# Fused decode step on Trainium2: TensorE's code begins behind 350 products that never run, and 256 rows of W_down go to 32 partitions by four small transfers

## The chip, the cores and the metric

The kernel runs on one core of one Trainium2 chip. The metric is the device time of one execution in microseconds; lower is better. A core has five engines that follow their own instruction streams: TensorE (PE, with its weight loads listed apart as PEld), VectorE (DVE), ScalarE (ACT), GpSimd (POOL) and SyncE (SP), and 16 DMA engines that move data between the chip's memory (HBM) and the on-chip buffer.

## The reference

One decode step for four sequences (B = 4, one token each, D = 512). A layer norm of x feeds two branches that are added to x.

```python
xn = _layernorm(x)
q = xn @ wq                      # 32 heads of 128, 8 key/value heads
scores = q @ k^T * Dh**-0.5      # the last 4096 positions of k_cache
o = softmax(scores) @ v
A = o.reshape(B, 1, 4096) @ wo
B_ = (silu(xn @ w_gate) * (xn @ w_up)) @ w_down   # F = 1792
return x + A + B_
```

All inputs are bfloat16. The 4,096 positions of 8 key/value heads and 4 sequences make 64 MiB of keys and values; the weights add 13 MiB.

## The kernel before, in words

**Transfers.** SP issues nearly every transfer, in one queue, in this order (L256 to L267): wq into the second V buffer, w_gate, w_up, then for each of the 8 key/value heads g the keys K(g) and the values V(g), 4 MiB each, into two buffers that take turns; the keys of the last head come in two halves. Behind V(7) come the transfers of W_down (L261 to L263), and behind these wo in five parts of 16, 8, 5, 2 and 1 row blocks (L265, L266). A transfer over 128 partitions is split over all 16 DMA engines, and its semaphore is complete when the last of them has landed its share. K(g) waits until the transposes of K(g-2) are done, V(g) until the products of V(g-2) are done; wo goes into the first K buffer once head 6's transposes are done.

**W_down.** F is 14 blocks of 128 rows. 13 of them (`NM = NF - 1`) go to `WD`, 128 partitions of 13 KiB, by one transfer (L261). The remaining 128 rows go to `WDX`, which lies where w_gate was: 16 partitions (`JX = 128 // NX`) with `NX = 8` rows each, by four transfers of four partitions, `WDX[o:JX:4]` for o = 0 to 3 (L262, L263). Each partition takes 8 KiB. TensorE waits for all five with one wait (L483) and multiplies the 13 blocks in `down` (L482) and the 8 rows of each of 16 partitions in `down_rest` (L487).

**TensorE's code.** It is written out instruction by instruction and follows this order: 4 transposes of xn (L377), 128 products for q (L384), 84 products for the gate and 84 for the up projection (L396; NM + NX = 21 groups of NC = 4), then a loop over pairs of heads (L491) whose body holds both heads of a pair, then the tail (L523 to L545). A product is two instructions, a weight load and a multiplication. The code holds about 1,080 products: 300 ahead of the loop, 696 in the loop's body, 84 in the tail. The loop runs four times.

**A head in the loop.** 16 chunks of 8 transposes of K (L415), evicted by DVE (L326) and ACT (L280), 16 chunks of 8 score products (L427), the maximum (L332 to L340), its subtraction (L439), the exponential on ACT (L283), and the products with V (L448, L454). `spin` (L468) issues products whose result nobody reads; `warm` calls it in the gaps at the softmax.

**The tail.** `fin` (L459) closes the last head; `down`; four products that permute the result (L528), which wait for DVE's `norm` (L345 to L352); `down_rest`; then wo. Its first 16 row blocks go into four row groups of one bank (L538), which ACT copies (L298); the other 16 go straight into the result (L540), each part after the wait for its transfer (L535). DVE and ACT copy the result (L370, L300) and ACT's queue stores it (L302).

Of the kernel before, what the change touches and what calls it, by code (L numbers as in the profile page):

```python
# [10 lines left out]
def bass_parallel_sum__sliding_block_cached__swiglu_ffn__decode_kernel(  # L11
# [12 lines left out]
    B, _, D = A_x.shape  # L24
    _, HKV, Sk, Dh = A_k_cache.shape
# [5 lines left out]
    NF = F // 128  # L31
# [15 lines left out]
    WOS = (0, 16, 24, 29, 31, 32)  # L47
    WOE = 16
    NR = HQ * Dh // 128

    NM = NF - 1
    FM = 128 * NM
    NX = 8
    JX = 128 // NX

    def sb(name, shape, dtype, align=32):
        return nc.alloc_sbuf_tensor(name, shape, dtype, align_bytes=align)
# [8 lines left out]
    WU = sb("wu_sb", [128, NC, F], BF16, 512)  # L66
    WD = sb("wd_sb", [128, NM, D], BF16, 512)
    WO = KB[0][:].rearrange("p t d -> p (t d)").rearrange("p (r n) -> p r n", r=NR)

    WDX = WG[0:JX].rearrange("p c f -> p (c f)")[:, 0:NX * D].rearrange("p (m n) -> p m n", n=D)  # L70
    X = sb("x_sb", [B, D], BF16, 512)
# [22 lines left out]

    OP = sb("oP", [128, NR, 32], BF16)
    S2 = sb("s2", [128, D], FP32)
    ex = sb("ex", [128, NM + NX, B], FP32)
    gs = sb("gs", [128, NM + NX, B], FP32)
    guT = sb("guT", [128, NM + NX, 32], BF16)
    ident = sb("ident", [128, 128], BF16)  # L100
    ones = sb("ones", [128, 128], BF16)
    I4 = sb("i4", [B, B], FP32)
    own = sb("own", [128, 128], BF16)
# [3 lines left out]
    dq = sb("dq", [128, 4], FP32)  # L107
    dr = sb("dr", [128, NR], BF16)
    sel = sb("sel", [128, 32], FP32)
# [4 lines left out]
    ps_kt = [ps("ps_kt%d" % s, [128, 512], FP32) for s in range(3)]  # L114
# [12 lines left out]
    q_ps = ps_S[0][:, 0:HQ * B]  # L127
    gate_ps = ps_O[:, 64:64 + (NM + NX) * B].rearrange("p (t b) -> p t b", b=B)
    up_ps = ps_O[:, 192:192 + (NM + NX) * B].rearrange("p (t b) -> p t b", b=B)
# [3 lines left out]
    acc4_ps = ps_S[1]  # L133
    perm_ps = [ps_kt[h][:, 0:B // 2 * NR] for h in (2, 0)]

# [49 lines left out]
    wdx_ap = B_w_down[0:F - FM].rearrange("(i o m) n -> o i m n", o=4, m=NX)  # L185
    wo_ap = A_wo.rearrange("(p r) n -> p r n", r=NR)

# [47 lines left out]
    def on_sync(eng):  # L235
# [26 lines left out]
        for o in range(4):  # L262
            eng.dma_start(WDX[o:JX:4], wdx_ap[o]).then_inc(d_wd, 16)  # L263
        eng.wait_ge(s_tr[NCH - 1], HKV - 1)
# [106 lines left out]

    def on_tensor(eng):
        mm = eng.matmul
        eng.wait_ge(s_const, 1)
        eng.wait_ge(s_xn, 1)
        for c in range(NC):
# [10 lines left out]
        for w, d, o in ((WG, d_wg, gate_ps), (WU, d_wu, up_ps)):  # L387
            eng.wait_ge(d, 16)
            for t in range(NM + NX):
                for c in range(NC):  # L390
                    if t < NM:
                        left = w[:, :, F - FM:F].rearrange("p c (m t) -> p c t m", t=NM)[:, c, t, :]
                    else:
# [4 lines left out]
                              skip_group_check=True)  # L398
# [60 lines left out]
        def fin(n):  # L459
# [4 lines left out]
                last = mm(O2_ps, Osb[:, Dh * h:Dh * (h + 1)], sel[:, NH * h:NH * (h + 1)],  # L464
                          start=(h == 0), stop=(h == 1), skip_group_check=True)
            last.then_inc(s_fin, 1)

        def spin(n, k=2):  # L468
            for _ in range(n):
                mm(ps_kt[k][:], ones[:], own[:].unsqueeze(1).to_broadcast([128, 4, 128]),  # L470
                   skip_group_check=True)

        def acc4(n, left, right, start, stop):
            return mm(acc4_ps[32 * n:32 * n + 32, :], left, right, start=start, stop=stop, skip_group_check=True)  # L474
# [12 lines left out]
        def down_rest():  # L487
            for m in range(NX):
                acc4(m % 4, guT[0:JX, NM + m, :], WDX[:, m, :], False, False)

        with eng.Fori(1, HKV + 1, 2) as m:  # L491

            d = eng.snap((m - 1) * 8 + 16)
            for u in range(2):
                n = m if u == 0 else eng.snap(m + 1)
                n1 = eng.snap(n + 1)

                def warm(k, bank=2):

                    if u:  # L500
                        spin(k, bank)
                    else:
                        with eng.If(m > 1):
                            spin(k, bank)
                for c in range(NCH):
                    transposes(u, c, n, d)
                    if c == 2:
                        fin(n)
                    if c >= 2:
                        scores(c - 2, n)  # L510
                scores(NCH - 2, n)
                scores(NCH - 1, n)
                warm(5)
                maxima(n)
                warm(5)
                shift(n)
                eng.wait_ge(d_v[u], d)
                pv(u, n1)
                if u == 0:
                    with eng.If(m < HKV - 1):  # L520
                        warm(4, 1)

        spin(2, 1)  # L523
        fin(HKV + 1)
        down()
        eng.wait_ge(s_nrm, HKV + 1)
        for b in range(B):
            last = mm(perm_ps[b // 2][:, NR * (b % 2):NR * (b % 2 + 1)], OT[:, b, 2:HKV + 2].rearrange("p k h q -> p (k h q)"), dr[:])  # L528
        last.then_inc(s_pm, 1)
# [22 lines left out]
    on_scalar(nc.scalar)  # L552
    on_vector(nc.vector)
    on_tensor(nc.tensor)

# [26 lines left out]
```

## Time and profile before

| | |
|---|---|
| median of 3 runs | 195.12 us (195.11 to 195.25) |
| the profiled execution's own time | 195.3 us |
| its span in the trace | 193.9 us |
| granted TensorE clock | 0.991 |
| PE busy / DVE / ACT | 163.8 / 99.0 / 69.1 us |
| HBM read | 81.01 MB, 418 GB/s over the span |
| DMA packets of data on SP's queue | 3776 |
| DMA packets of instructions | 8 |

The span runs from the first to the last instruction that the trace holds; 1.4 us of the execution lie around it. In the DMA view a window of the trace lists the packets that start in it, and how many of them are under 512 B. Each of the DMA engines that serve a transfer ends its share with a packet of 4 B, the write of the semaphore; the count under 512 B in a short window is therefore the number of engines that end a transfer there.

### The profile page before, as it was taken

How to read it: one execution, taken by the hardware profiler on the slowest of the kernel's cores; microseconds unless marked ns; L12 is line 12 of the kernel's file. 1: busy time of each engine (PE TensorE's matmuls, PEld its weight loads, DVE VectorE, ACT ScalarE, POOL GpSimd, SP SyncE). 2: the span in 40 equal slices, each digit the busy share in tenths (PEclk: the TensorE clock that was granted, in tenths of full speed). 3: DMA queues.
4: the chain of work that ended last, by engine and by line, in shares of the span. 5: the costliest groups of instructions: out<-in, count | busy, mean ns of one | idle time of the engine just before them, and what ended most of it. 6: DMA issues, size and time to landing. Idle time of an engine off the chain costs nothing.

```text
span 193.9 us, 6951 instructions
## 1 busy us (share of the span) xinstructions
PE 163.8 (84%) x3179; PEld 135.2 (70%) x3179; DVE 99.0 (51%) x200; ACT 69.1 (36%) x100; POOL 5.7 (3%) x33
## 2 busy tenths in 40 slices
PE   0038973998699899999999799989996999999995
PEld 0038973997389759956994699469945994997532
DVE  0200011578258737870885188428842884588230
ACT  5510000243416343525461446234623462363421
POOL 7300000000000000000000000000000000000000
PEclk9999999999789999999999999999999999999999
DMA  6999999999999999999999999999999999999993
GB/s 216 433 438 429 427 429 433 429 433 429 433 429 436 426 429 436 426 433 433 439 433 433 433 433 433 433 433 433 433 433 433 433 426 433 439 433 433 436 400 131
DMA packets 3800, 81.14 MB, mean 418 GB/s; under 512 B 440, under 2 KB 576, under 8 KB 832
## 3 DMA queue, kind: packets, MB, share of 16 engines
q1 hardware_dynamic: 3776, 81.00, 97.5%
q8 instruction: 8, 0.13, 0.2%
q10 hardware_dynamic: 16, 0.01, 0.0%
HBM read 81.01 MB, written 0.00 MB: 418 GB/s over the span
## 4 chain that ended last, share of the span: by engine, by line
PE 48%; DMA 44%; DVE 5%; issue 1%; SPq 1%; ACT 0%; DVEq 0%
DMA kbuf<-in_A_k_cache_dram 44%; PE ps_kt L415 23%; PE ps_s L427 8%; PE ps_o L448 5%; PE ps_kt L470 4%; DVE kT L326 2%; PE ps_s L439 2%; PE ps_s L464 2%; DVE mx L332 2%; PE ps_s L478 1%; PE ps_s L474 1%; PE ps_s L461 1%; PE ps_kt L454 1%; PE ps_kt L434 0%; ACT s L298 0%
## 5 line engine op out<-in xcount | busy, mean ns | idle before, releaser
L415 PE MATMUL ps_kt<-ident,kbuf 128*128 128x128 bf16 x1024 | 78.2, 224 | 9.0 <-DMA kbuf<-in_A_k_cache_dram 8.5
L415 PEld LDWEIGHTS ps_kt<-ident,kbuf 128*128 128x128 bf16 x1024 | 60.6, 100 | 11.2 <-DMA kbuf<-in_A_k_cache_dram 9.6
L326 DVE COPY kT<-ps_kt 128x1024 bf16<-128x1024 bf16 x88 | 57.6, 686 | 18.5 <-PE ps_kt L415 16.5
L280 ACT ACTIVATE kT<-ps_kt 128x1024 bf16<-128x1024 bf16 x40 | 40.9, 1023 | 52.9 <-PE ps_kt L415 52.9
L427 PE MATMUL ps_s<-qC,kT 128*128 128x16 bf16 x1024 | 44.8, 170 | 2.6 <-DVE kT L326 1.9
L427 PEld LDWEIGHTS ps_s<-qC,kT 128*128 128x128 bf16 x1024 | 38.4, 97 | 4.6 <-DVE kT L326 4.1
L283 ACT ACTIVATE p<-ps_s 128x512 bf16<-128x512 f32 x32 | 16.5, 603 | 34.0 <-PE ps_s L439 34.0
L332 DVE TENSOR_REDUCE mx<-ps_s 128x16 f32<-128x512 f32 x32 | 22.0, 689 | 6.9 <-PE ps_s L427 5.0
L470 PE MATMUL ps_kt<-own,ones 128*128 128x512 bf16 x82 | 20.7, 380 | 0.0
L448 PE MATMUL ps_o<-vbuf,p 128*32 128x256 bf16 x512 | 19.1, 289 | 0.3
L448 PEld LDWEIGHTS ps_o<-vbuf,p 128*32 128x32 bf16 x512 | 14.9, 101 | 5.9 <-ACT p L283 4.2
L343 DVE TENSOR_REDUCE dsum<-ps_kt 128x16 f32<-128x256 f32 x8 | 3.4, 425 | 28.6 <-PE ps_kt L454 28.6
L454 PE MATMUL ps_kt<-p,ones 128*32 128x256 bf16 x64 | 16.9, 287 | 0.0
L470 PEld LDWEIGHTS ps_kt<-own,ones 128*128 128x128 bf16 x82 | 6.6, 97 | 7.0 <-issue 1.1
L377 PE MATMUL ps_s<-i,xn 4*128 4x4 f32 x4 | 0.6, 254 | 10.1 <-DVE xn L312 10.1
L439 PE MATMUL ps_s<-cm,own 128*128 128x512 bf16 x32 | 8.3, 380 | 1.0 <-DVE cm L340 1.0
L377 PEld LDWEIGHTS ps_s<-i,xn 4*128 4x128 f32 x4 | 0.6, 208 | 10.1 <-issue 10.1
L454 PEld LDWEIGHTS ps_kt<-p,ones 128*32 128x32 bf16 x64 | 6.6, 103 | 0.1
L290 ACT ACTIVATE ex<-ps_o 128x84 f32<-128x84 f32 x1 | 0.2, 240 | 17.5 <-PE ps_o L396 17.5
L439 PEld LDWEIGHTS ps_s<-cm,own 128*128 128x128 bf16 x32 | 2.5, 97 | 5.3 <-DVE cm L340 3.4
L286 ACT ACTIVATE osb<-ps_o 128x256 f32<-128x256 f32 x8 | 3.1, 383 | 8.2 <-PE ps_kt L454 8.2
L464 PE MATMUL ps_s<-sel,osb 128*128 128x16 f32 x36 | 5.8, 275 | 0.0
(83 smaller groups left out, 84.8 us busy)
## 6 DMA issues: line engine op xcount, KB each, us to landing
vbuf<-in_A_v_cache_dram SPq DMA_DIRECT2D x8, 4096.0 KB, 30.5
kbuf<-in_A_k_cache_dram SPq DMA_DIRECT2D x7, 4096.0 KB, 27.4
vbuf<-in_A_wq_dram SPq DMA_DIRECT2D x1, 4096.0 KB, 12.4
kbuf<-in_A_k_cache_dram SPq DMA_DIRECT2D x2, 2048.0 KB, 25.3
kbuf<-in_A_wo_dram SPq DMA_DIRECT2D x1, 2048.0 KB, 27.2
wg_sb<-in_B_w_gate_dram SPq DMA_DIRECT2D x1, 1792.0 KB, 16.1
wu_sb<-in_B_w_up_dram SPq DMA_DIRECT2D x1, 1792.0 KB, 20.9
wd_sb<-in_B_w_down_dram SPq DMA_DIRECT2D x1, 1664.0 KB
```

Of the source, the lines that this page charges most:

```text
L280: eng.activation(KT[:, c % 4], kt_ps[c % 3], ACT.Copy).then_inc(s_ev[c], 1)
L283: eng.activation(P[:, BT * q:BT * (q + 1), :], ps_S[q][:].rearrange("p (t n) -> p t n", n=NH), ACT.Exp, scale=SCALE).then_inc(s_p[q], 1)
L326: eng.tensor_copy(KT[:, c % 4], kt_ps[c % 3]).then_inc(s_ev[c], 1)
L332: eng.tensor_reduce(mx[:, q, :], ps_S[q][:].rearrange("p (t n) -> p n t", n=NH), AX.X, ALU.max)
L343: eng.tensor_reduce(dsum[:], den_ps.rearrange("p (t n) -> p n t", n=NH), AX.X, ALU.add).then_inc(s_dn, 1)
L415: last = eng.transpose(kt_ps[c % 3][:, k, :], KB[u][:, CH * c + k, :], ident[:])
L427: last = mm(ps_S[q][:, NH * t:NH * (t + 1)], KT[:, c % 4, k, :], QC[:], start=(t == 0), stop=False, skip_group_check=True)
L439: mm(ps_S[q][:].rearrange("p (t n) -> p t n", n=NH), own[:], CM[:].unsqueeze(1).to_broadcast([128, BT, NH]), start=False, stop=True, skip_ ...
L448: mm(O_ps[32 * n:32 * n + 32, :], P[:, t:t + 2, :].rearrange("p t n -> p (t n)"), VB[u][:, t:t + 2, :].rearrange("p t d -> p (t d)"), star ...
L454: last = mm(den_ps[32 * n:32 * n + 32, :], ones[:, 0:32], P[:, DT * e:DT * (e + 1), :].rearrange("p t n -> p (t n)"), start=(e < 4), stop= ...
L464: last = mm(O2_ps, Osb[:, Dh * h:Dh * (h + 1)], sel[:, NH * h:NH * (h + 1)], start=(h == 0), stop=(h == 1), skip_group_check=True)
L470: mm(ps_kt[k][:], ones[:], own[:].unsqueeze(1).to_broadcast([128, 4, 128]), skip_group_check=True)
```

## The change

- 256 rows of W_down instead of 128 go to `WDX`: `NM` falls from 13 to 12, `JX` rises from 16 to 32. `WD` takes 12 KiB on each of 128 partitions; each of the four small transfers now has 8 partitions of 8 KiB. The bytes in all are the same.
- The groups of the gate and up projections fall from 21 to 20 (80 products each instead of 84), those of `down` from 13 to 12; `down_rest` keeps 8 products, on 32 partitions instead of 16.
- TensorE's code begins with a register set to 0, a branch on it, and `ROOM = 350` products that the branch jumps over: 700 instructions that never run. `spin` is defined ahead of them instead of further down. All code behind them lies 700 odd instructions further on.

```diff
-    NM = NF - 1
+    ROOM = 350
+
+    NM = NF - 2
     FM = 128 * NM
     NX = 8
-    JX = 128 // NX
+    JX = 256 // NX
...
     def on_tensor(eng):
         mm = eng.matmul
+
+        def spin(n, k=2):
+            for _ in range(n):
+                mm(ps_kt[k][:], ones[:], own[:].unsqueeze(1).to_broadcast([128, 4, 128]),
+                   skip_group_check=True)
+
+        zero = eng.alloc_register("never")
+        eng.reg_mov(zero, 0)
+        with eng.If(eng.snap(zero) > 0):
+            spin(ROOM)
         eng.wait_ge(s_const, 1)
```

More of the change, by code (lines that the diff above doesn't have):

```diff
@@ L466, in fin @@
             last.then_inc(s_fin, 1)
[L468 to L471, printed above, removed]
         def acc4(n, left, right, start, stop):
```

## The prediction

> **What bounds the kernel now.** I read the page's slices and queues first, then the chain of waits, then the DMA view in windows. From the page:
>
> ```profile
> span 193.9 us, 6951 instructions
> ...
> GB/s 216 433 438 429 427 429 433 429 433 429 433 429 436 426 429 436 426 433 433 439 433 433 433 433 433 433 433 433 433 433 433 433 426 433 439 433 433 436 400 131
> DMA packets 3800, 81.14 MB, mean 418 GB/s; under 512 B 440, under 2 KB 576, under 8 KB 832
> ...
> q8 instruction: 8, 0.13, 0.2%
> ```
>
> The transfers run at 433 GB/s from the first slice to the last but one, 27.1 GB/s for each of 16 DMA engines; nothing that only makes an engine faster can shorten that. Eight packets of 16 KB are instructions. The chain of waits, and the one wait of the tail that matters:
>
> ```profile
> 0.81 0.39 SPq L256
> ...
> 83.81 26.45 DMA kbuf<-in_A_k_cache_dram
> ...
> 120.96 28.01 DMA kbuf<-in_A_k_cache_dram
> 149.01 1.51 PE ps_kt L415 x24
> ...
> 189.61 2.54 PE ps_s L478 x36
> ...
> PEld ps_s L478 <- DMA kbuf<-in_A_wo_dram: 0.4, 2, 0.2
> ```
>
> PE waits for keys until 110.3 and again until 149.0; from there it works almost without a gap into the last products of wo (L478), and there it waits for wo twice, 0.4 us in all. So the end hangs on two things of nearly equal length: the last landing of wo, after which only L478's last pair, the copy and the store are left, and PE's own work since 149.0, which is at most 0.4 us shorter. A later last landing moves the end one to one; an earlier one can win 0.4 us at most.
>
> The last landing is that of the slowest of 16 DMA engines, so I ask how far they lie apart. The instruction queue in the windows 15 to 28, 28 to 40 and 15 to 80 us, a row from each:
>
> ```profile
> q8 instruction: 2, 0.03, 0.9%
> q8 instruction: 1, 0.02, 0.5%
> q8 instruction: 8, 0.13, 0.7%
> ```
>
> All eight come between 15 and 80 us, while PE goes through its code for the first time, none in the later passes: fetched code stays. About 2,230 instructions (1,080 products of two, and some 70 others) in the eight blocks fetched and a first one or two present at the start make some 220 to 250 a block of 16 KB. Then how many engines end a transfer in a window (the count under 512 B): wq in 12.1 to 12.6 and 12.6 to 12.9; V(0) in 40.0 to 40.5, 41.5 to 41.8 and 42.1 to 42.2; V(7) in 175.6 to 176.0, 176.0 to 177.1, 177.1 to 177.5 and 177.6 to 177.8; wo's first part in 184.5 to 184.8, 185.7 to 186.3 and 186.5 to 186.6; a row from each:
>
> ```profile
> DMA packets 30, 0.22 MB, mean 430 GB/s; under 512 B 15, under 2 KB 15, under 8 KB 15
> DMA packets 11, 0.14 MB, mean 478 GB/s; under 512 B 1, under 2 KB 1, under 8 KB 1
> DMA packets 28, 0.49 MB, mean 983 GB/s; under 512 B 13, under 2 KB 13, under 8 KB 13
> DMA packets 8, 0.20 MB, mean 655 GB/s; under 512 B 2, under 2 KB 2, under 8 KB 2
> DMA packets 2, 0.03 MB, mean 328 GB/s; under 512 B 1, under 2 KB 1, under 8 KB 1
> DMA packets 19, 0.20 MB, mean 512 GB/s; under 512 B 8, under 2 KB 8, under 8 KB 8
> DMA packets 21, 0.38 MB, mean 343 GB/s; under 512 B 0, under 2 KB 0, under 8 KB 0
> DMA packets 22, 0.20 MB, mean 499 GB/s; under 512 B 7, under 2 KB 7, under 8 KB 7
> DMA packets 11, 0.13 MB, mean 666 GB/s; under 512 B 1, under 2 KB 1, under 8 KB 1
> DMA packets 16, 0.16 MB, mean 546 GB/s; under 512 B 4, under 2 KB 4, under 8 KB 4
> DMA packets 37, 0.22 MB, mean 369 GB/s; under 512 B 11, under 2 KB 11, under 8 KB 11
> DMA packets 11, 0.08 MB, mean 819 GB/s; under 512 B 1, under 2 KB 1, under 8 KB 1
> ```
>
> This carries everything that follows. Before any fetch the engines end wq together, one of them, call it S, some 0.3 us behind. After three fetches three engines are 1.4 us late at V(0), and the last of them, alone at 42.1, is S: the third fetch was on S. After eight fetches eight engines are late by 1.4 us, S last again. So each fetch holds up one engine, each a different one, by **1.4 us, and it is never made good**, for no engine is ever idle. Behind the W_down transfers only four engines are still early: the four small transfers lie on four engines without a fetch. The page's 440 packets under 512 B say so too: 26 transfers on 16 engines (416), x and the output on 4 each (8), which leaves 16 for four transfers, 4 engines each. 32 KB more on these four cost them 1.2 us, which just filled their lead.
>
> **The change, part by part.**
>
> *W_down.* Durations are of the profiled execution (195.3 us, span 193.9, so 1.4 us around it; the median of the runs is 0.2 us lower).
>
> ```profile
> wd_sb<-in_B_w_down_dram SPq DMA_DIRECT2D x1, 1664.0 KB
> ...
> wg_sb<-in_B_w_down_dram SPq DMA_DIRECT2D x4, 32.0 KB
> ```
>
> The large transfer becomes 1,536 KB: 8 KB less on each engine, 8 / 27.1 = -0.30 us. The small ones become 64 KB each. By the pattern of four partitions on four engines I take eight on eight: 32 KB on each of eight engines, +1.21 us, four of them new. No row shows eight; what another spread would do is a rival.
>
> *The code.* PE jumps over 700 instructions, some three blocks, as soon as the kernel begins; SP, which starts with it, issues its first transfer at 0.81 us (row above), so I put the jump at about 1 us. The block it lands in, and the next, were not fetched before, since the blocks present at the start lie at the front. So they are fetched at once, between about 1 and 6 us. PE itself loses nothing:
>
> ```profile
> PE ps_s L377 <- DVE xn L312: 10.1, 1, 10.1
> ...
> PEld ps_kt L528 <- DVE oT L352: 0.4, 1, 0.4
> ...
> 0.00:1.80 1.80, 0.00 (x0) 0.00 (x0) 0.00 (x0) 0.00 (x0) 1.08 (x14) 1.00 0.00 0
> 1.80:2.20 0.40, 0.00 (x0) 0.00 (x0) 0.00 (x0) 0.00 (x0) 0.22 (x2) 1.00 3.60 983
> ```
>
> It waits for xn until 10.1 us anyway. Without that cover a stall of one fetch, a few us, would be paid once. But the data stream begins at 1.8 to 2.2 us, so the two fetches meet it. Their price is the unknown: nothing, if they get in ahead; 16 KB at 27.1 GB/s, 0.61 us; or 1.4 us as for the eight others. I take 1.4, the row it is nearest to: two more fetches on a busy engine. Then come the fetches of the first pass as before, from the prologue into the tail: some eight. Ten in all instead of eight, and some eight engines with extra rows, on 16 engines: at least two engines have both. The early fetch of the second block lands on S: by block (S's was the third one fetched before, the fifth of the code if two are present at the start; the landing in the fourth makes the fifth the next) as well as by the order of fetches, give or take one.
>
> [...]
>
> *The sum.* S carried one fetch before and carries one after. If it is among the eight: -0.30 + 1.21 = **+0.91 us**. S ended last before, so the end moves by this: span 194.8, the execution 196.2, on the median 195.12 + 0.91 = **196.0 us**. PE's own chain is no help: K(6) on S is as late as before, so head 6 starts at 149.0 again.
>
> *What lies beside other work.* Four gate and four up products fewer end before K(0) has landed. `down` has 12 products instead of 13 while the next step waits 0.4 us for DVE's oT (row above): nothing won. K(0) on S comes some 0.4 us after the other late engines, so head 0 starts later by that; the 26.45 us wait for keys that ends at 110.3 takes it up. SP's four issues stay where they were, 30 us ahead of their landing. Were these covers gone, each would cost 0.1 to 0.4 us.
>
> **The rivals.**
>
> *Another engine than S has both.* The eight engines with a fetch avoided the first four. If they follow each other, there are five places for them, and S lies within the first eight in two. In the other three an engine that ended 0.3 to 0.5 us ahead of S gets the +0.91, or one of the first four trades 8 KB for a fetch: -0.30 + 1.4, from 0.6 to 0.8 us ahead. Both end +0.3 to +0.6: 195.4 to 195.7. [...]
>
> *The early fetches cost half*, 0.61: S then is at -0.30 + 1.21 - 1.4 + 0.6 = +0.1: 195.2, no measurable change.
>
> *The other side: they cost nothing.* Ahead of the stream, an early fetch leaves S without a late one, and if all later ones fall on the eight without extra rows, S moves by -0.30 + 1.21 - 1.4 = -0.5, the others by -0.30. K(6) would land 0.3 earlier too, and PE's chain with it, so about -0.4 of it reaches the end: 194.7. It decides from an early fetch under 0.5 us on S. For it: the branch comes at about 1 us, the stream at 1.8. Against: the jump and the stream's start lie within a microsecond of each other, and S's block is the second to be fetched.
>
> *The change does not do what it says*: the small transfers are spread otherwise (all 16 engines: S -0.30 + 0.61 = +0.3; the same four: +0.1 to +0.3): 195.2 to 195.4.
>
> *The loop's code no longer stays* and is fetched again in each pass: one or more 1.4 us on an engine per pass, over 197.
>
> **How the numbers follow.** A measurement of this kernel tells about 0.2%, 0.4 us, from no change. Chances: S with both 0.36; another engine with both 0.24; half price 0.15; free 0.15; spread otherwise 0.06; fetched in each pass 0.04. Slower by over 0.2%: 0.36 + 0.22 + 0.04 = 0.62. Within: 0.15 + 0.06 + 0.02 + 0.03 of the free case = 0.26. Faster: 0.12. The range takes in the bounds of the early fetch, nothing (194.7) to 1.4 us, with 0.3 us for its size above: 194.7 to 196.3.
>
> **What would show it.** Right: ten or so instruction packets, two of them before 8 us; 456 packets under 512 B on the page; two engines late at wq, one of them S near 14.2; two engines alone at the end of wo, some 0.9 us behind the rest. Wrong: no instruction packet before 15 us, or sixteen engines that end wq within 0.7 us; wo's end with all engines within 0.5 us; packets of instructions after 80 us ahead of the tail.

## The result and the profile after

| | before | after |
|---|---|---|
| median of 6 runs each | 195.19 us (195.11 to 195.35) | 196.3 us (196.15 to 196.34) |
| ratio | | 1.0055 [1.0045, 1.0066] |
| the profiled execution's own time | 195.3 us | 196.34 us |
| its span | 193.9 us | 194.9 us |

The kernel became 1.1 us slower. The page of the changed kernel, its head and its queue of instructions:

```profile
span 194.9 us, 6936 instructions
...
DMA packets 3834, 81.18 MB, mean 416 GB/s; under 512 B 456, under 2 KB 592, under 8 KB 848
...
q8 instruction: 10, 0.16, 0.3%
```

Ten packets of instructions instead of eight, and 456 packets under 512 B instead of 440: each of the four small transfers now ends on eight engines. When the instructions were fetched, by the DMA view of the changed kernel in the windows 0 to 15, 15 to 80 and 80 to 194 us:

```profile
q8 instruction: 2, 0.03, 0.8%
q8 instruction: 7, 0.11, 0.6%
q8 instruction: 1, 0.02, 0.1%
```

Two come ahead of 15 us (at 3.9 and 10.2), seven by the end of the loop's first pass at 73 us (two of these ahead of the loop, whose first products start at 32.7 us), and one in the tail (between 189 and 190 us). The same view tells how many engines end a transfer in a window: wq in 12.0 to 12.9, 13.75 to 13.85 and 14.0 to 14.2; V(7) in 175.5 to 176.3, 177.1 to 177.6 and 178.6 to 178.8; the last part of wo in 191.9 to 192.1 and 192.4 to 192.5 (the count under 512 B):

```profile
DMA packets 35, 0.34 MB, mean 376 GB/s; under 512 B 14, under 2 KB 14, under 8 KB 14
DMA packets 3, 0.03 MB, mean 287 GB/s; under 512 B 1, under 2 KB 1, under 8 KB 1
DMA packets 8, 0.10 MB, mean 502 GB/s; under 512 B 1, under 2 KB 1, under 8 KB 1
...
DMA packets 26, 0.36 MB, mean 456 GB/s; under 512 B 8, under 2 KB 8, under 8 KB 8
DMA packets 26, 0.25 MB, mean 508 GB/s; under 512 B 7, under 2 KB 7, under 8 KB 7
DMA packets 10, 0.11 MB, mean 553 GB/s; under 512 B 1, under 2 KB 1, under 8 KB 1
...
DMA packets 12, 0.01 MB, mean 61 GB/s; under 512 B 2, under 2 KB 10, under 8 KB 12
DMA packets 2, 0.00 MB, mean 10 GB/s; under 512 B 1, under 2 KB 2, under 8 KB 2
```

The first group shows the two early fetches: two engines end wq 1.4 us or so behind the fourteen others. So an early fetch costs what a late one costs. The packets of the trace show what the 1.4 us is made of: a packet of code takes 0.88 to 0.97 us on its engine, and the packet of keys, values or weights right behind it takes 1.67 to 1.76 us instead of 1.21 (32 KB). The second group shows what the prediction did not have. By the end of V(7) nine fetches have come, but eight engines are still early; seven are 1.4 us late and one, alone at 178.7, is late by twice that. The ninth fetch fell on an engine that had been held up already. The packets can be followed engine by engine, for in this full stream a packet starts 3 or 4 ns before the one ahead of it on its engine ends. Followed so, the late one is the engine of the first fetch. The tenth, in the tail, falls on that of the second, and this engine is the last of all at the end of wo, alone at 192.47.

The chain of waits of the changed kernel, for the windows 80 to 195 us:

```profile
83.90 27.32 DMA kbuf<-in_A_k_cache_dram
111.27 1.51 PE ps_kt L426 x24
...
121.93 27.95 DMA kbuf<-in_A_k_cache_dram
149.93 1.51 PE ps_kt L426 x24
...
190.53 2.65 PE ps_s L484 x36
```

L426 and L484 are L415 and L478 of before. Head 6 begins at 149.93 instead of 149.01, for the engine with two fetches lands its share of K(6) last. These +0.92 us stay in PE's chain to the first product of L484: 190.53 instead of 189.61, +0.92. And the waits for wo of the changed kernel:

```profile
PEld ps_s L484 <- DMA kbuf<-in_A_wo_dram: 0.7, 3, 0.2
```

0.7 us instead of 0.4 us, some of it on the path: L484 takes 2.65 us to the end of its run instead of 2.54. So of the 1.0 us by which the span grew, 0.9 were there 30 us before the rows of W_down came, and 0.1 came in the tail.

### The profile page after: what moved, and what is told of

It is laid out like the page before. It is cut to its first block, busy times and chain, and to the rows that moved or that the text cites. A ratio compares the mean times of both kernels' runs of the same rounds, so it can differ in the third digit from the quotient of the medians.

```text
span 194.9 us, 6936 instructions
## 1 busy us (share of the span) xinstructions
PE 162.6 (83%) x3170; PEld 133.5 (69%) x3170; DVE 98.8 (51%) x200; ACT 69.2 (35%) x100; POOL 5.7 (3%) x33
## 4 chain that ended last, share of the span: by engine, by line
PE 48%; DMA 44%; DVE 4%; issue 1%; SPq 1%; ACT 0%; DVEq 0%
DMA kbuf<-in_A_k_cache_dram 44%; PE ps_kt L426 23%; PE ps_s L438 9%; PE ps_o L459 4%; PE ps_kt L378 4%; PE ps_s L450 2%; DVE kT L327 2%; PE ps_s L475 2%; PE ps_s L484 1%; DVE mx L333 1%; PE ps_s L472 1%; PE ps_s L480 1%; PE ps_kt L465 1%; PE ps_kt L445 0%; ACT s L299 0%
## 5 line engine op out<-in xcount | busy, mean ns | idle before, releaser
L426 PE MATMUL ps_kt<-ident,kbuf 128*128 128x128 bf16 x1024 | 77.8, 223 | 9.0 <-DMA kbuf<-in_A_k_cache_dram 8.9
L426 PEld LDWEIGHTS ps_kt<-ident,kbuf 128*128 128x128 bf16 x1024 | 60.2, 99 | 12.4 <-DMA kbuf<-in_A_k_cache_dram 10.5
L459 PEld LDWEIGHTS ps_o<-vbuf,p 128*32 128x32 bf16 x512 | 14.3, 97 | 5.8 <-ACT p L284 4.6
L459 PE MATMUL ps_o<-vbuf,p 128*32 128x256 bf16 x512 | 18.0, 278 | 0.3
L465 PE MATMUL ps_kt<-p,ones 128*32 128x256 bf16 x64 | 15.9, 276 | 0.0
L450 PE MATMUL ps_s<-cm,own 128*128 128x512 bf16 x32 | 9.1, 411 | 1.0 <-DVE cm L341 1.0
L388 PE MATMUL ps_s<-i,xn 4*128 4x4 f32 x4 | 0.6, 254 | 10.6 <-DVE xn L313 10.6
L388 PEld LDWEIGHTS ps_s<-i,xn 4*128 4x128 f32 x4 | 0.6, 208 | 10.6 <-issue 10.6
L395 PE MATMUL ps_s<-xnT,vbuf 128*128 128x4 bf16 x128 | 3.6, 166 | 3.4 <-DMA vbuf<-in_A_wq_dram 3.4
L395 PEld LDWEIGHTS ps_s<-xnT,vbuf 128*128 128x128 bf16 x128 | 3.5, 104 | 3.5 <-issue 3.5
```

Of the source, the lines that this page charges most:

```text
L395: last = mm(q_ps[:, h * B:(h + 1) * B], WQ[:, c, h * Dh:(h + 1) * Dh], XnT[:, c, :], start=(c == 0 and h == 0), stop=(c == NC - 1), skip_g ...
L426: last = eng.transpose(kt_ps[c % 3][:, k, :], KB[u][:, CH * c + k, :], ident[:])
L450: mm(ps_S[q][:].rearrange("p (t n) -> p t n", n=NH), own[:], CM[:].unsqueeze(1).to_broadcast([128, BT, NH]), start=False, stop=True, skip_ ...
L459: mm(O_ps[32 * n:32 * n + 32, :], P[:, t:t + 2, :].rearrange("p t n -> p (t n)"), VB[u][:, t:t + 2, :].rearrange("p t d -> p (t d)"), star ...
L465: last = mm(den_ps[32 * n:32 * n + 32, :], ones[:, 0:32], P[:, DT * e:DT * (e + 1), :].rearrange("p t n -> p (t n)"), start=(e < 4), stop= ...
```

## The experiments

Two theories stood at first. A: the two extra fetches, on engines that had one already, make all of it, and the rows of W_down are hidden. B: the rows on a fetched engine make it. A third, C, stands in the expectations of the shorter branches: the price lies in the jump itself and its two fetches at the start of the stream. All kernels were timed beside the kernel before; unless stated otherwise the diffs are against it, and `...` stands for lines left out.

**Each half alone.** The first with the rows and no branch, the second with the branch and 128 rows:

```diff
-    NM = NF - 1
+    NM = NF - 2
...
-    JX = 128 // NX
+    JX = 256 // NX
```

> The 256 rows on 32 partitions, without the branch and the 350 products. Theory A (fetches of code go round eight engines; the eight that get the extra rows never have one; what cost 1.1 us is a ninth and a tenth fetch): eight instruction packets, all after 15 us; eight engines early by 1.4 us until the W_down transfers and level with the rest behind them; every engine that ended last before has 8 KB less, -0.30 us, of which PE's own chain lets 0.2 to 0.3 through: 194.9 us (194.8 to 195.1). Theory B (as the prediction had it: extra rows meet a fetched engine): some engine has both, +0.3 to +0.9: 195.5 to 196.1.

```diff
+        zero = eng.alloc_register("never")
+        eng.reg_mov(zero, 0)
+        with eng.If(eng.snap(zero) > 0):
+            spin(ROOM)          # ROOM = 350
```

> The branch and the 350 products with 128 rows on 16 partitions, as before. Theory A: ten instruction packets, two ahead of 15 us; two engines with two fetches, one of them in time to hold up the keys; 196.6 us, that is the changed kernel and the 0.30 us that 8 KB less per engine saved there (196.4 to 196.9). Theory B: no new rows on a fetched engine, so only one late start: at most 195.6.

The rows alone: 195.83 us (195.68 to 195.87), ratio 1.0034 [1.0021, 1.0046]; here A failed and B was right, also in size. The branch alone: 196.45 us (196.2 to 196.65), 1.0061 [1.0046, 1.0077]; here A was right. Each half costs by itself, and the two together no more than the branch alone. Why, is read from the rows alone, first by the engines that end V(7) in 175.5 to 176.2 and 177.1 to 177.9, then by those that end the first part of wo, behind W_down, in 184.2 to 184.7 and 186.9 to 187.05:

```profile
DMA packets 26, 0.36 MB, mean 521 GB/s; under 512 B 8, under 2 KB 8, under 8 KB 8
DMA packets 37, 0.36 MB, mean 445 GB/s; under 512 B 8, under 2 KB 8, under 8 KB 8
...
DMA packets 15, 0.19 MB, mean 377 GB/s; under 512 B 2, under 2 KB 2, under 8 KB 2
DMA packets 11, 0.07 MB, mean 471 GB/s; under 512 B 2, under 2 KB 2, under 8 KB 3
```

Eight engines carry a fetch as in the kernel before. Behind W_down only two engines are still early, and two are late alone: eight with a fetch and eight with rows, on sixteen engines, leave two with neither and two with both. The chain of waits of the rows alone, windows 80 to 195 us:

```profile
121.03 28.00 DMA kbuf<-in_A_k_cache_dram
149.08 1.51 PE ps_kt L415 x24
...
160.60 30.76 DMA kbuf<-in_A_wo_dram
191.40 1.27 PE ps_s L478 x16
```

Head 6 starts as early as before (149.08), and the end is set by the landing of wo. In the branch alone it is the other way round. Its chain in 80 to 195 us, and, in the DMA view, the engines that end V(7) in 177.0 to 177.7 and 178.9 to 179.0:

```profile
122.19 27.96 DMA kbuf<-in_A_k_cache_dram
150.20 1.51 PE ps_kt L426 x24
```

```profile
DMA packets 27, 0.27 MB, mean 380 GB/s; under 512 B 7, under 2 KB 7, under 8 KB 7
DMA packets 5, 0.05 MB, mean 533 GB/s; under 512 B 1, under 2 KB 1, under 8 KB 1
```

Again seven engines with one fetch and one with two, and head 6 late by 1.2 us. So the changed kernel holds two delays of which the larger counts: one engine with two fetches, 1.4 us later than with one, by which head 6 and everything behind it come 0.9 to 1.2 us later, and two engines with a fetch and rows, +0.9 us at wo. The end goes by the maximum and not by the sum.

**How far the code has to move.** Fewer products behind the same branch, 128 rows: 4 (nothing but the branch itself), 110, and later 135. This diff is against the branch alone:

```diff
-    ROOM = 350
+    ROOM = 4            # then 110, then 135
```

> As before with a branch over 4 products, code that grows by 13 instructions. Theory A: eight packets that matter, 195.2 us, no change. Theory C in a form in which the branch itself costs: slower than 195.4.

> As before with a branch over 110 products: the code begins in its second block, which is there at the start, and ends one block later. Theory A: nine instruction packets, all after 15 us; the ninth, at about 76 us, falls on the engine of the first, which then is 2.8 us late, 0.7 to 1.0 us behind the last one of before from the keys of 78 us on: 195.9 to 196.2 us. A third theory, C (the price lies in the jump and its two fetches at the start of the stream): no such fetch, 195.2 us.

> As the kernel before with a branch over 135 products, 50 instructions more than with 110, so that the loop reaches 75 instructions into its last block instead of some 25. If a block is asked for only some way into the one ahead of it, the ninth packet now comes at about 76 us and not at 152, the keys are held up as well, and the time is 196.0 to 196.5; if the ninth packet stays at 152 us its place has another reason.

With 4 products: 195.25 us (195.09 to 195.41, 10 runs), 1.0002 [0.9993, 1.0011], eight packets of instructions, head 6 at 149.13. The jump itself costs nothing, so that part of C falls. With 110: 196.24 us (196.12 to 196.45), 1.0058 [1.0043, 1.0074], within a little of what A said, but not by the way that it said. In the DMA view the instruction packets in 0 to 15, 15 to 80 and 151 to 153 us, and the engines that end V(7) in 178.5 to 178.6:

```profile
q8 instruction: 1, 0.02, 0.4%
q8 instruction: 7, 0.11, 0.6%
q8 instruction: 1, 0.02, 3.0%
...
DMA packets 5, 0.05 MB, mean 533 GB/s; under 512 B 1, under 2 KB 1, under 8 KB 1
```

I had put all fetches into the stream and the ninth at 76 us. One came at 5 us, and the ninth only at 151.7 us, in the last pass of the loop, whose code had been there for three passes. It too fell on an engine that had one already, the one that ends V(7) alone at 178.5 to 178.6. Its chain in 80 to 195 us:

```profile
121.34 27.60 DMA kbuf<-in_A_k_cache_dram
148.99 1.51 PE ps_kt L426 x24
...
160.51 31.14 DMA kbuf<-in_A_wo_dram
191.70 1.27 PE ps_s L484 x16
```

Behind the ninth fetch there is no key transfer left to be held up; head 6 starts at 148.99, and the end is set by wo's landing instead. With 25 products more the ninth comes at 75 to 78 us; the instruction packets of that window, the engines that end V(7) in 178.8 to 179.0, and the chain in 80 to 195 us:

```profile
q8 instruction: 1, 0.02, 2.0%
...
DMA packets 7, 0.08 MB, mean 399 GB/s; under 512 B 1, under 2 KB 1, under 8 KB 1
```

```profile
122.16 27.95 DMA kbuf<-in_A_k_cache_dram
150.16 1.51 PE ps_kt L426 x24
```

196.3 us (196.23 to 196.49), 1.0058 [1.0043, 1.0073]: the same time as with 110 products, since an engine late by two fetches, 2.8 us, holds up either head 6 or the last of wo. Both kernels fetch nine blocks in all, and a ninth costs 1.1 us whether it comes at 76 or at 152 us. That 50 instructions more bring the ninth packet 75 us forward was forecast from the thought that a block is asked for only when PE is some way into the one ahead of it. The forecast came true, but it does not show the thought, for with 110 products the last pass asked for a block that three passes through the same code had not. What the packets do show is that in these kernels the last packet of code comes shortly after a jump back to the loop's start: with 135 products 2.4 us into the second pass (75.8, the pass begins at 73.4), with 110 products 2.7 us into the last (151.7 and 149.0), and in the kernel before 3.4 us into the second (76.5 and 73.1). Why it is the second pass there and the last one here stays open.

**Rows only where no fetch falls.** If the eight engines with a fetch are always the same ones, rows on six others should cost nothing (D). Three spreads were tried, two of them also with the branch; all take 256 rows, so `NM` and the waits change with them:

```diff
...
-        for o in range(4):
-            eng.dma_start(WDX[o:JX:4], wdx_ap[o]).then_inc(d_wd, 16)
+        for o in range(5):
+            eng.dma_start(WDX[o:30:5], wdx_ap[o]).then_inc(d_wd, 16)
+        eng.dma_start(WDX[30:JX], wdy_ap).then_inc(d_wd, 16)
```

> The 256 rows on 32 partitions without the branch, but by five transfers of six partitions and one of two instead of four of eight, so that six DMA engines share them instead of eight (40 KB each, two of them 48 KB). Theory D (of the first eight engines, two are among those that fetch code; the extra rows cost only where they meet a fetch, and the first six never do): no engine has both; the last one is the laggard with its one fetch and 8 KB less than before: 194.9 to 195.1 us, at least 0.6 below the eight-engine form. Rival E (more rows in small transfers cost as such, wherever they land): 195.6 or more.

> The changed kernel, branch and 350 products included, with the same five and one transfers. Theory D: the slowest engines are then the two with two fetches alone, which had no extra rows, and the end is set by the slowest engine, not by a sum: 196.2 to 196.4 us, no change against the changed kernel. Rival F (the two costs add up in the changed kernel): about 0.5 less, 195.8.

The rows in five transfers of six partitions and one of two: 199.22 us (199.1 to 200.07), 1.0215 [1.0197, 1.0234], where 194.9 to 195.1 was expected. With the branch: 199.96 us (198.81 to 201.36), 1.0262 [1.0212, 1.0312]. Neither says anything about D, for something else broke: the transfers became slow. I asked whether it is the partitions, which here lie five apart and not four, with eight neighbouring partitions in each of four transfers; the rival cause of the slow form is the six engines or the odd transfer of two:

```diff
...
-    wdx_ap = B_w_down[0:F - FM].rearrange("(i o m) n -> o i m n", o=4, m=NX)
+    wdx_ap = B_w_down[0:F - FM].rearrange("(o i m) n -> o i m n", o=4, m=NX)
...
-            eng.dma_start(WDX[o:JX:4], wdx_ap[o]).then_inc(d_wd, 16)
+            eng.dma_start(WDX[8 * o:8 * o + 8], wdx_ap[o]).then_inc(d_wd, 16)
```

> The 256 rows without the branch on eight engines, each transfer on eight neighbouring partitions instead of eight that lie four apart. [...] Rival (six engines or the odd transfer of two made it slow): as the eight-engine form, 195.8.

198.95 us (198.3 to 200.27), 1.0205 [1.0167, 1.0243], with the same bytes on the same number of engines as the rows alone, which had 195.83. The windows view, 179.4 to 184.8 us, where W_down and its rows run, last column GB/s: the rows four apart, then the rows five apart, then neighbours:

```profile
179.40:184.80 5.40, 5.34 (x87) 2.79 (x85) 1.40 (x5) 2.55 (x6) 0.00 (x0) 1.00 1.02 436
```

```profile
179.40:184.80 5.40, 5.34 (x87) 2.71 (x85) 1.46 (x5) 2.55 (x6) 0.00 (x0) 1.00 1.04 376
```

```profile
179.40:184.80 5.40, 5.36 (x87) 3.04 (x88) 1.20 (x4) 2.55 (x6) 0.00 (x0) 1.00 1.04 288
```

The share of busy time stays at 1.02 to 1.04 and the rate falls to 288 GB/s: the packets take longer. With neighbours those of 8 KB take 0.31 to 0.89 us, half of them over 0.5, instead of 0.31 for all; W_down's other packets (12 KB) and wo's (16 KB) are stretched too, to at most 1.0 us instead of 0.46 and 1.2 us instead of 0.61. The time is as high as with the rows five apart (198.95 against 199.22), so six engines are not needed for it, and the rival's 195.8 failed. But this form also reads the rows in another order from HBM (the other half of its diff), so that the cause lies in the partitions is likely and not shown. For a third spread I kept the partitions four apart: 192 rows by four transfers of six partitions (8 KB each) and 64 rows by four of four partitions (4 KB each), 24 groups in the gate and up projections. First without the branch, then with it:

```diff
...
-    JX = 128 // NX
+    JX = 24
+    NY = 4
+    JY = 64 // NY
...
+        for o in range(4):
+            eng.dma_start(WDY[o:JY:4], wdy_ap[o]).then_inc(d_wd, 16)
```

> The 256 rows without the branch, again on six DMA engines, but every engine writes partitions four apart as in the eight-engine form: 192 rows by four transfers of six partitions of 8 KB, 64 rows by four of four partitions of 4 KB (48 KB on four engines, 32 KB on two). Theory D (rows cost only on an engine that fetches code, and the first six do not): 0.31 us for every 8 KB packet, no engine with a fetch and rows, 194.9 to 195.2 us, 0.6 or more below the eight-engine form's 195.83. Theory E (extra rows in small transfers cost wherever they land): 195.6 or more.

> The changed kernel, branch included, with the rows on six engines four partitions apart. If the end is set by the slowest engine alone, and that is one with two fetches and no extra rows: 196.2 to 196.6 us, no change. If the costs of rows and of fetches add: 195.8 or less.

Without the branch 195.85 us (195.66 to 196.03), 1.0038 [1.0024, 1.0052]: as fast as the rows four apart on eight engines (195.83), and D failed. The engines that end the first part of wo in 184.2 to 184.5, in 186.85 to 187.0, and its last part in 191.9 to 192.0:

```profile
DMA packets 10, 0.09 MB, mean 300 GB/s; under 512 B 3, under 2 KB 3, under 8 KB 3
DMA packets 9, 0.06 MB, mean 416 GB/s; under 512 B 1, under 2 KB 1, under 8 KB 2
...
DMA packets 1, 0.00 MB, mean 0 GB/s; under 512 B 1, under 2 KB 1, under 8 KB 1
```

Three engines are early now and one is late alone, so, if the spread begins on the same engine, one of the two that had both is still among its first six places, the other was in the seventh or eighth. (This kernel's code is longer, and a ninth packet of instructions comes at 191 us; the engine that is late alone was so at 186.9 already.) With the branch 196.57 us (196.42 to 196.72), 1.0073 [1.0058, 1.0089], as expected: rows placed better help nothing while engines with two fetches are last (two of them here, as the tenth packet comes at 73 us). No kernel of the study is faster than the one before.

**Which engine the ninth fetch takes.** Either the order of the fetches decides, or the block of the code. With the 350 products behind gate and up instead of at the start, 128 rows, the first blocks are fetched as before and three in the middle are passed over:

```diff
+        zero = eng.alloc_register("never")
+        eng.reg_mov(zero, 0)
+        with eng.If(eng.snap(zero) > 0):
+            spin(ROOM)          # between the up projection and the loop
```

> As the kernel before, but with the branch over 350 products between the gate and up projections and the loop. Blocks counted from 0, of 256 instructions with some 56 ahead of the kernel's own (from the place of the fetches in the other runs): 2 and 3 are fetched in the prologue, 5 and 6 by the jump, 7 to 11 in the loop's first pass, 12 in the tail; ten in all. Which engine fetches a block: by its number, counted round eight, block 10 falls on the engine of block 2 and block 11 on that of block 3, so that after the keys of about 78 us seven engines are late and two of these twice; by the order of the fetches, the ninth (block 11) falls on the engine of the first, eight engines are late and one of these twice. Both give 196.0 to 196.6 us; the count of engines that end a transfer early (nine or eight) tells them apart.

196.47 us (196.34 to 196.65), 1.0062 [1.0046, 1.0079], ten fetches, the first at 19 us: the price is the same without an early fetch, so the other part of C falls too. The engines that end w_up in 22.55 to 22.65, by when there has been one fetch; those that end K(0) in 32.05 to 32.2 and in 32.2 to 32.35, by when two engines have been held up; and V(7) in 177.36 to 177.38 and 178.95 to 178.99:

```profile
DMA packets 2, 0.03 MB, mean 328 GB/s; under 512 B 1, under 2 KB 1, under 8 KB 1
...
DMA packets 3, 0.07 MB, mean 434 GB/s; under 512 B 1, under 2 KB 1, under 8 KB 1
DMA packets 2, 0.03 MB, mean 218 GB/s; under 512 B 1, under 2 KB 1, under 8 KB 1
...
DMA packets 2, 0.01 MB, mean 666 GB/s; under 512 B 1, under 2 KB 1, under 8 KB 1
DMA packets 4, 0.04 MB, mean 998 GB/s; under 512 B 1, under 2 KB 1, under 8 KB 1
```

One engine is late twice here too, so the count goes by order. The packets say which. The engine of the first fetch ends w_up at 22.60 us, alone behind the fifteen others, and K(0), eight packets further, at 32.28: it is the later of the two. The engine of the second fetch ends K(0) at 32.11. An engine without a fetch takes 145.26 us from the end of K(0) to that of V(7). So does the engine of the second fetch, which ends V(7) at 177.37; that of the first takes 1.43 us more and ends it last, at 178.97. So the ninth fetch falls on the engine of the first, by order and not by the number of the block. The tenth of the changed kernel goes by the same order: it fell on the engine of the second.

Its chain in 24 to 36 us shows what a jump in mid-stream does to PE:

```profile
2.18 30.50 DMA kbuf<-in_A_k_cache_dram
32.68 2.51 issue
35.18 0.92 PE ps_kt L426 x7
```

K(0) has landed at 32.68 and PE stands 2.5 us more; in every other kernel of the study the first transposes start at 32.4 to 32.9 us, here at 35.18. The time is no worse than with the branch at the start, since the later waits for keys take this up (head 6 starts at 150.22 here and at 150.20 there).

## Why the prediction was right and where it failed

*The time* was forecast at 196.0 us and is 196.3, above the median of before by 1.1 us instead of 0.91. The direction holds, and the range of 194.7 to 196.3 holds at its upper end. That the time came so near is luck, as the sum below shows.

*What stood.* A fetch costs 1.4 us on one engine, an early one no less than a late one; the half price and the free case fall with the two engines that end wq at 13.8 and 14.1. Ten fetches, two of them early, though the second came at 10.2 us and not before 8. Eight engines with rows, -0.30 + 1.21 us, and two engines with rows and a fetch: the rows alone show it with 2 early and 2 late engines, and with +0.67 us on the median. The jump itself costs nothing (4 products: ratio 1.0002; with 350 PE waits for xn until 10.6 us, as it waited until 10.1 before). The loop's code does stay, but the reading behind it was a little off: of the eight fetches in 15 to 80 us the last, at 76.5, lies in the loop's second pass, which begins at 73.1.

*The step that failed* is "each fetch holds up one engine, each a different one", which was read from eight fetches and carried over to ten. The runs show fetches on eight engines only; a ninth goes back to one of them. So "Ten in all instead of eight, and some eight engines with extra rows, on 16 engines: at least two engines have both" comes out at two, but from eight and eight engines, not from ten and eight: it needed no branch. With it failed "K(6) on S is as late as before, so head 6 starts at 149.0 again": it starts at 149.93, for the engine of the ninth fetch is late twice. None of the rivals had this either.

*S.* S was to decide as the engine that ends last by 0.3 us. In the changed kernel no engine is that far behind the others in wq before a fetch: the fourteen without one end by 12.9. Who is last was decided by the number of fetches instead.

*The sum* came within 0.2 us of the measured difference with a wrong term in it: +0.91 for a fetched engine with rows at the end of wo stood in for +0.92 at K(6) by two fetches on one engine, with 0.1 us for wo in the tail. The forecast term does exist in the changed kernel, but engines that carry it end at 191.9 to 192.1, behind which the double engines end at 192.2 and 192.47. So two engines are alone at the end of wo, as the prediction's signs wanted it, but not the two that it meant. For a change with the branch alone the same steps would have shown no engine behind S, and no time lost; it costs 1.2 us.

*What stays open.* Eight engines fetch code in the kernel before, and in the changed one the ninth packet (70.7 us) goes to the engine of the first and the tenth (189.1 us) to that of the second. Why eight, and what gives a packet its engine, no run shows. Nor does any show why the stream moves 436 GB/s while the rows lie four apart, and 376 five apart and 288 with neighbours: none changed the partitions that an engine writes with all else equal.

## What to carry to other kernels

In a kernel whose DMA engines are never idle, count what each single engine carries, the code too: a block of instructions is 16 KB on one engine, 1.4 us late there until the end, and moving code by a few hundred instructions can add such a block (here 1.1 us with 110 products or more, nothing with 4). Delays on different engines do not add up: the end takes the largest (195.83 us with the rows alone, 196.45 with the branch alone, 196.3 with both), so a fix for one shows nothing while another is as large, and a sum can come out right with the wrong engine in it. A pattern read from eight cases says nothing of the ninth; look for what could run out (here engines that fetch code) before carrying it further.

## What the runs showed of the hardware that was not expected

- Fetches of TensorE's code went over eight of the 16 DMA engines, in turn: in the changed kernel the ninth, at 70.7 us, fell on the engine of the first, which was then late twice (178.7 us at V(7), against 177.1 to 177.6 for once), and the tenth, at 189.1, on that of the second; with the branch ahead of the loop the ninth fell on the engine of the first too (178.97 us, against 177.37).
- A packet of code of 16 KB cost its engine 1.4 us and not the 0.61 that its bytes take at the engine's rate: 0.88 to 0.97 us for itself, and about 0.5 us by which the next packet was longer.
- A packet of code can come shortly after the jump back to the loop's start, and not in each pass: 2.4 us into the second pass with 135 products ahead (75.8 us), 2.7 us into the fourth with 110 (151.7 us).
- While the small transfers of 8 KB per partition run, the stream moves 436 GB/s with their partitions four apart, 376 five apart and 288 with neighbours; neighbours cost 3.1 us against four apart (198.95 against 195.83).
- With a jump ahead of the loop PE stood 2.51 us beyond the landing of its keys, at 32.68; with the jump ahead of all data the first transposes of the keys start at 32.7 us.
